# Loading the first MLP rows and weights during the last recurrent segments, and computing six of their products in the free slots of the last block, with two changed priorities

## The chip, the cores and the metric

The kernel runs on one core of one Trainium2 chip. The metric is the device time of one execution in microseconds (us). A run counts as slow when it is over 1.5% above the fastest run of its kernel.

Engines are named as in the profile: PE is TensorE (matmuls), PEld its weight loads, DVE is VectorE, ACT is ScalarE, POOL is GpSimd, SP is the engine that issues the DMA transfers. "L931" is line 931 of the kernel concerned. The lines differ between the two kernels, so a small key goes with each profile.

## The reference, cut to what matters

```python
x = A_x                                            # 1 x 2048 x 512, bfloat16
h = x + A(_layernorm(x), mem0, Wq, Wk, Wv, Wo)     # recurrent attention
h2 = h + B(_layernorm(h), w1, b1, w2, b2)          # MLP 512 -> 1792 -> 512

def A(x, mem, ...):                                # 32 heads of 128
    for s in range(64):                            # 64 segments of 32 tokens
        hs = concat([mem, x[32 * s : 32 * s + 32]])   # 8 memory rows + 32 tokens
        q, k, v = hs @ Wq, hs @ Wk, hs @ Wv
        o = softmax(mask(q @ k.T * scale)) @ v @ Wo
        mem = o[:8]                                # goes on to the next segment
        out[s] = o[8:]

def B(y, ...):
    return gelu(y @ w1 + b1) @ w2 + b2             # gelu: tanh form
```

The attention is a chain of 64 segments that can't overlap freely, because each needs the memory rows of the one before. The MLP of a row needs only that row's `h`, so the MLP of the first rows could start long before the last segment is done. Four segments (128 tokens) make a block, so there are blocks 0 to 15 and block 15 is segments 60 to 63.

Of the kernel before, what the change touches and what calls it, by code (L numbers as in the profile page):

```python
# [24 lines left out]
PHASE = (87, 24, 172, 102)  # L25
HALVES = ("kq", "KA", "QT", "ZCm", "VS", "nmc", "EC", "rsc", "PC", "PTC", "OTm", "KB", "QTB", "VSB")
BONUS = {"EC0": 9.64, "EC1": 2.52, "KA1": 1.19, "KB0": -4.21, "KB1": 40, "OTB": -40, "OTm0": 25.44, "OTm1": -8.14, "OTx": 40, "PA": -3.16, "PC0": 2.46, "PC1":
         4.62, "PTA": -4.05, "PTC0": -40, "PTC1": 2.94, "QT0": -2.59, "QT1": 6.99, "QTB0": 6.21, "QTB1": -0.93, "SA": -13.03, "TT": 6.79, "VBD": 1.92,
         "VS0": 0.75, "VS1": -11.93, "VSB0": -5.47, "VSB1": 15.43, "WK": 40, "WQ": 1.54, "WV": 2.9, "ZCb": 0.16, "ZCm0": 40, "ZCm1": -3.19, "ag":
         -4.83, "ag2": 40, "b1n": 6.73, "b1t": -6.81, "b2bc": 40, "cneg": -40, "hB": 3.99, "hTm": -5.4, "hTx": 5.79, "hd": -2.53, "kq0": 4.71, "kq1":  # L30
         12.67, "kq2": 10.08, "kq5": 6.67, "maskA": -7.3, "maskAF": -11.82, "maskCF": -12.78, "maskL": 40, "maskR": 2.12, "nma": -4.99, "nmc0": 40,
         "nmc1": 40, "oN": -40, "opA": 4.9, "opB": -1.91, "rs": 40, "rs2": -8.34, "rsa": -1.22, "rsc0": -3.89, "rsc1": -3.1, "sma": -4.13, "st2": -40,
         "vd": -1.71, "xT": 0.29, "xn": -0.19, "xr": 3.08}
# [3 lines left out]

# [9 lines left out]
class Op:  # L47
    __slots__ = ("eng", "fn", "reads", "writes", "idx", "gidx", "deps", "sig", "sigcount", "waits",
                 "tag", "pad", "name", "is_dma", "dma_sem", "dur", "mode", "rank", "start", "succ", "prev", "ni", "dma_count", "alts", "kind")

    def __init__(self, eng, fn, reads, writes, name, dur, mode):
# [3 lines left out]
        self.tag = self.pad = None  # L55
# [11 lines left out]
class Sched:  # L67
# [235 lines left out]
    def align(self):  # L303

        at, seg, owed, late = FETCH_AT, 0, 0, 0
        for o in self.streams["pe"]:
            at += len(o.waits) // 2
            if PHASE and o.tag is not None and o.tag[0] != seg:
                seg = o.tag[0]
                owed = (PHASE[seg % 4] - at) % FETCH_N  # L310
                if owed > FETCH_N - SLIP:
                    owed = 0
            if o.pad is not None and owed > 0:
                o.pad[0] = min(owed, PADS)
                owed -= o.pad[0]
            at += o.ni + (o.pad[0] if o.pad is not None else 0)
# [55 lines left out]
P = 128  # L372
# [5 lines left out]
DC = 4  # L378
# [10 lines left out]
MC, MR, MF = 1, 2, 3  # L389

# [25 lines left out]
def build_kernel(nc, A_x, A_mem0, A_Wq, A_Wk, A_Wv, A_Wo, B_w1, B_b1, B_w2, B_b2, out):  # L416
# [3 lines left out]
    with st:  # L420
# [209 lines left out]
        def one_pass(lhs, reads, W, key, r, bank, rhs):  # L630

            for cc in range(DC):
                pad = [0]

                def f(e, cc=cc, pad=pad):
                    for j in range(4):
                        for _ in range(j, pad[0], 4):
                            e.ldweights(lhs(cc), tile_position=(0, 32 * j))
                        ins = e.matmul(ps[bank][32 * j:32 * j + 32, :], lhs(cc), rhs(W, r, cc, j), start=(cc == 0), stop=(cc == DC - 1), tile_position=(0, 32 * j))  # L639
                    return ins  # L640
                S.op("pe", f, reads=[(key, r, cc)] + reads, writes=[("ps", bank)], dur=0.215, mode=MC, ni=8).pad = pad

        def two_passes(lhs, reads, parts):

            for cc in range(DC):
                pad = [0]

                def f(e, cc=cc, pad=pad):
                    for n, (W, _, r, bank, rhs) in enumerate(parts):
                        for j in range(4):  # L650
                            o, l, m = ps[bank][32 * j:32 * j + 32, :], lhs(cc), rhs(W, r, cc, j)
                            if n == 0:
                                for _ in range(4 + j, pad[0], 4):
                                    e.ldweights(l, tile_position=(0, 32 * j))
                            if n == 0 or j < pad[0]:
                                ins = e.matmul(o, l, m, start=(cc == 0), stop=(cc == DC - 1), tile_position=(0, 32 * j))
                            else:
                                ins = matmul_kept(e, o, l, m, cc == 0, cc == DC - 1, (0, 32 * j), (P, 32))
                    return ins
                S.op("pe", f, reads=[(key, r, cc) for _, key, r, _, _ in parts] + reads, writes=[("ps", p[3]) for p in parts], dur=0.43, mode=MC, ni=12).pad = pad  # L660
# [15 lines left out]
        def pack_a(s):  # L676
            sl = s % RING
            return (lambda cc: hT[:, sl, cc, :]), [("hTx", (s // 4) % RBLK), ("hTm", sl)]

        def pack_b(bk):  # L680
            return (lambda cc: hB[:, bk % RBLK, cc, :]), [("hB", bk % RBLK)]
# [45 lines left out]
        def kq_B(bk, qk, r, bank):  # L727
            W, key = WKQ[qk]
            one_pass(*pack_b(bk), W, key, r, bank, cols_kq)
            kq_B_out(bk, qk, r, bank)  # L730

        def v_B(bk, r, bank):
            one_pass(*pack_b(bk), WV, "WV", r, bank, cols_v)
# [245 lines left out]
        hx0, xn0 = xr[:, 2:6, :], view(hT, 4 * DC * SEG, [P, TBS, D])  # L979
        used = {"WQ": [], "WK": [], "WV": []}  # L980

        def hx_of(k):
            return hx0 if k == 0 else hx2[:, k % 2]

        def xn_of(k):
            return xn0 if k == 0 else xn2[:, k % 2]
# [7 lines left out]
        def p2_load(k):  # L994
            after = S.users([("xr", i) for i in range(2, 6)]) if k == 0 else used["WQ"]
            S.dma(lambda e: e.dma_start(hx_of(k), hd[:, k * TBS:(k + 1) * TBS, :]), 512, reads=[("hd", k * TBS + t) for t in range(TBS)],
                  writes=[("hx", bf_of(k))], after=after)

        def p2_norm(k):
            after = S.users([("hTx", i) for i in range(1, RBLK)] + [("hTm", i) for i in range(4, RING)]) if k == 0 else used["WV"]  # L1000
            for t in range(TBS):
                tb = k * TBS + t
                S.op("dve", lambda e, tb=tb, t=t: e.tensor_scalar(xn_of(k)[:, t, :], hx_of(k)[:, t, :], agg2[:, tb, 0:1], rst2[:, tb:tb + 1], ALU.subtract, ALU.mult),
                     reads=[("hx", bf_of(k)), ("ag2", tb), ("rs2", tb)], writes=[("xn4", bf_of(k), t)], after=after, dur=0.4)

        def p2_res(k):

            for t in range(TBS):
                S.op("pool", lambda e, t=t: e.tensor_tensor(hb[:, k % 2, t, :], hx_of(k)[:, t, :], b2bc[:], ALU.add), reads=[("hx", bf_of(k)), "b2bc"],
                     writes=[("hb", k % 2, t)], after=used["WV"] + S.users([("rs2", NTB - 1)]), dur=1.1)  # L1010

        def p2_T(k):
            for t in range(TBS):
                S.dma(lambda e, t=t: e.dma_start_transpose(hnT_of(k)[:, :, t * P:(t + 1) * P], xn_of(k)[:, t, :]), 256, reads=[("xn4", bf_of(k), t)],
                      writes=[("hnT", bf_of(k), t)], after=[] if k == 0 else used["WQ"])
# [8 lines left out]
        ln1(0)  # L1024
        for s in range(NS):
# [7 lines left out]
            if s == NS - 4:  # L1033
                p2_load(0)
                p2_norm(0)
                p2_T(0)

            def part_F2():
                banks = BANK["F0"], BANK["F1"]
                if 0 < bk < NTB - 1 and sg < 3:  # L1040
                    W, key, cols = ((WK, "WK", cols_kq), (WQ, "WQ", cols_kq), (WV, "WV", cols_v))[sg]
                    two_passes(*pack_b(bk + 1), [(W, key, r, banks[r], cols) for r in range(2)])
# [8 lines left out]
            def part_F(r):  # L1051
                if sg < 2 and 0 < bk < NTB - 1:
                    kq_B(bk + 1, sg, r, BANK["F%d" % r])
                if sg == 2 and 0 < bk < NTB - 1:
                    v_B(bk + 1, r, BANK["F%d" % r])
                if sg == 3 and bk > 0 and r == 1:
                    wo_B(bk - 1, BANK["FB"])

            late, done = [], []
# [15 lines left out]
            def part(name):  # L1075
                r = int(name[-1]) if name[-1].isdigit() else 0
                if name in ("K0", "K1"):
                    one_pass(*pack_a(s), WK, "WK", r, bank_of[name], cols_kq)
                    k_seg(s, r, bank_of[name])
                elif name in ("Q0", "Q1"):  # L1080
                    one_pass(*pack_a(s), WQ, "WQ", r, bank_of[name], cols_kq)
                    q_seg(s, r, bank_of[name])
                elif name in ("QK0", "QK1"):
                    two_passes(*pack_a(s), [(WQ, "WQ", r, bank_of["Q%d" % r], cols_kq), (WK, "WK", r, bank_of["K%d" % r], cols_kq)])
                    q_seg(s, r, bank_of["Q%d" % r])
                    k_seg(s, r, bank_of["K%d" % r])
                elif name == "V":
                    two_passes(*pack_a(s), [(WV, "WV", r, bank_of["V%d" % r], cols_v) for r in range(2)])
# [214 lines left out]
```

## The kernel before: what the change and the argument touch

The kernel is not written in the order in which the engines run it. Each operation is recorded, and a static list scheduler then fixes every engine's order before the program is built. An operation is named by the tile that it writes first ("kind"), and a table of priorities, `BONUS`, is added to its rank. The rank is the scheduler's own estimate, in us, of the longest path from the operation to the end.

```python
BONUS = {"EC0": 9.64, ..., "OTB": -40, ..., "st2": -40, ..., "xn": -0.19, "xr": 3.08}
...
        for o in topo:
            o.rank = o.dur + max([self.lat(o, s) + s.rank for s in o.succ], default=0.0)
        def push(o):      # only when all that o depends on has been popped
            heapq.heappush(heap, (-o.rank - BONUS.get(o.kind, 0.0), pos[o], o.gidx, o))
```

So `"OTB": -40` says: give the copies that write the tile OTB their places as if they were 40 us less urgent than they are. PE's own order is fixed by hand, part by part:

```python
ORDER = (("PVA", 0, 99), ("Q0", 0, 4), ("K0", 0, 4), ("Q1", 0, 4), ("K1", 0, 4), ("SC0", 0, 99), ("V0", 0, 4), ("V1", 0, 2), ("SC1", 0, 99), ("SA", 0, 99),
         ("V1", 2, 4), ("F0", 0, 2), ("PV0", 0, 99), ("F0", 2, 4), ("PV1", 0, 99), ("WO", 0, 8), ("F1", 0, 4))
...
            def part_F(r):
                if sg < 2 and 0 < bk < NTB - 1:
                    kq_B(bk + 1, sg, r, BANK["F%d" % r])     # next block's other rows: K, Q
                if sg == 2 and 0 < bk < NTB - 1:
                    v_B(bk + 1, r, BANK["F%d" % r])          # ... and V
                if sg == 3 and bk > 0 and r == 1:
                    wo_B(bk - 1, BANK["FB"])                 # output product of the block before, from OTB
```

`sg` is the segment's place in its block. `F0` and `F1` are filler: PE does the next block's projections there while the softmax of the segment (ACT and DVE) is on its way. Block 15 has no next block, so in segments 60 to 62 these slots are empty.

After a block's output product its rows go through `nat`: transpose, residual, row statistics, and a store to DRAM (`hd`). The input rows `xr` are in a ring of seven blocks:

```python
        def nat(bk):                                          # called at the start of block bk + 2
            S.dma(... dma_start_transpose(oN[:], opT[...]) ...)
            xs = xr[:, bk % XR, :]
            S.op("dve", ... tensor_tensor(xs, xs, oN, ALU.add) ...)
            S.op("dve", lambda e: e.bn_stats(st2[:, i, :], xs), reads=[("xr", bk % XR)], writes=[("st2", i)], ...)
            ...
            S.dma(lambda e: e.dma_start(hd[:, bk, :], xs), ...)
```

The MLP runs in four groups `k` of 512 rows: load the rows, normalize them, transpose them by DMA into `hnT`, multiply by W1 with GELU, multiply by W2. Group 0 borrows a part of the ring, and its load waits for all who use that part:

```python
        hx0, xn0 = xr[:, 2:6, :], view(hT, 4 * DC * SEG, [P, TBS, D])
        def p2_load(k):
            after = S.users([("xr", i) for i in range(2, 6)]) if k == 0 else used["WQ"]
            S.dma(lambda e: e.dma_start(hx_of(k), hd[:, k * TBS:(k + 1) * TBS, :]), 512, ..., after=after)
        def p2_norm(k): ...            # DVE
        def p2_T(k): ...               # four DMA transposes into hnT
        ...
            if s == NS - 4:            # at segment 60
                p2_load(0)
                p2_norm(0)
                p2_T(0)
```

W1 and W2 go into the place of the attention weights, so their loads wait until the last segment no longer needs those (`used["WK"]`), and the tail interleaves what is left of the attention (`rest`) with the first products:

```python
        rest = [lambda: wo(NS, 6, mem=False), lambda: pv_a(NS - 1), ..., lambda: wo(NS + 1, 7, mem=False), lambda: wo_B(NTB - 1, 6), ...]
        for k in range(NSB):
            ...                        # k == 0: one p2_w1 (4 matmuls and a GELU), one piece of rest, eight times
```

## Time and profile before

The median is 883.73 us (three runs, 883.22 to 884.57).

| part of the profiled run | us |
|---|---|
| span | 874.5 |
| start of segment 1 | 54.0 |
| segments 1 to 28 | 308.0 |
| segments 29 to 52 | 269.5 |
| segment 59, with the output product of a block in its F slots | 12.05 |
| segments 60, 61, 62 | 9.85, 11.30, 10.42 |
| start of segment 63 to the end of the span | 132.4 |

The table is worked out from the trace: a segment begins with the first matmul of its part PVA. This profiled run was a quick one: it took 876.2 us, and the timed ones 883 to 885.

Key to the lines of this kernel: L639 projections, L793 scores, L824 probabilities times V, L881 memory part (PVA), L909 output product WO, L1189 W1 products, L1196 W2 products, L948 row statistics of `nat`, L996 load of rows, L1014 transposes into `hnT`, L1207 and L1210 loads of W1 and W2.

First lines of the profile page of the kernel before: the span, the busy time of engines, PE's granted clock in tenths over 40 slices, and the chain of work that ended last.

```profile
span 874.5 us, 50672 instructions
...
PE 792.8 (91%) x22108; PEld 484.7 (55%) x24221; DVE 580.2 (66%) x1877; ACT 547.9 (63%) x1534; POOL 88.2 (10%) x205
...
PEclk9999999999999999999999999999999999789999
...
PE 83%; DVE 8%; issue 4%; DMA 3%; ACT 1%; SPq 1%; ACTq 0%; DVEq 0%
```

PE is busy 91% of the span and is 83% of the chain, so it bounds the kernel on average. The clock row has a hole (7, 8) in slices 35 and 36, around 760 us: this is the seam between the loop and the MLP.

The chain of waits of the kernel before, from 740 to 800 us, in order of time (start, duration, what):

```profile
750.83 1.97 PE ps L909 x67
752.80 2.90 issue
...
758.85 0.70 DVE st L948
...
759.77 1.32 SPq L1014
761.14 4.24 DMA hnT<-hT
...
765.90 1.48 PE ps L1189 x3
767.38 3.04 PE ps L909 x32
...
774.49 1.86 PE ps L909 x64
...
798.28 1.73 PE ps L1189 x8
```

After the last segment's WO (752.80) PE stands for 2.90 us without a wait that the profile shows ("issue"), then finishes 29 matmuls, then waits for the transposed rows. The work after that is slow: 3.04 us for a WO product that takes 1.86 us a little later. At 798.28 the first 512 rows are done and group 1 begins.

PE's waits between 700 and 800 us of the kernel before (who waited for whom, us in total, times, longest):

```profile
PE ps L1189 <- DMA hnT<-hT: 8.7, 1, 8.7
PE ps L909 <- issue: 4.5, 4, 2.9
```

The table of windows of the kernel before, same stretch (window, length, busy time and instructions of each engine, granted clock of PE, share of the DMA engines, GB/s):

```profile
700.00:800.00 100.00, 80.96 (x1896) 49.84 (x2196) 54.31 (x168) 48.58 (x129) 19.15 (x29) 0.93 0.38 93
```

PE is busy for 81 of 100 us here. The idle 19 us, and what is lost at half clock, are all that the change can hope for in this stretch.

### The profile page before, as it was taken

To read this page: it belongs to the slowest core of one execution; us is meant where nothing else is said; L and a number is where in the kernel's file an instruction comes from. 1 tells how busy PE (TensorE), PEld (TensorE's weight loads), DVE (VectorE), ACT (ScalarE), POOL (GpSimd) and SP (SyncE) were. 2 spreads that over 40 slices of the span, in tenths; PEclk is the share of its full clock that TensorE was granted. 3 is DMA by queue.
4 is the path that set the end of the run, shared out by engine and by line. 5 is a ranking of instruction groups with operands and counts; after the bars stand their busy time and mean duration, and the time that the engine had idled before them with its cause. 6 is when DMAs were issued, how large, how long until landed. Compare 5 with 4: busy or idle time off the path is not lost.

```text
span 874.5 us, 50672 instructions
## 1 busy us (share of the span) xinstructions
PE 792.8 (91%) x22108; PEld 484.7 (55%) x24221; DVE 580.2 (66%) x1877; ACT 547.9 (63%) x1534; POOL 88.2 (10%) x205
## 2 busy tenths in 40 slices
PE   3578999999999999999999899989998988499998
PEld 1255666666656665665656565655655655354443
DVE  3267777787777777777777777777877877532111
ACT  2357677777777777776767676767675767334342
POOL 4021000001000100010010001010101000015200
PEclk9999999999999999999999999999999999789999
DMA  9950010101010101010101101010202010951100
GB/s 357 362 168 16 5 28 16 35 17 34 17 34 16 35 16 34 17 34 16 35 22 28 28 22 29 22 34 15 42 17 39 11 40 5 244 96 49 49 24 25
DMA packets 61649, 46.65 MB, mean 53 GB/s; under 512 B 28276, under 2 KB 57852, under 8 KB 61436
## 3 DMA queue, kind: packets, MB, share of 16 engines
q1 hardware_dynamic: 61104, 43.14, 17.8%
q8 instruction: 182, 2.98, 1.4%
q14 instruction: 31, 0.25, 0.1%
q10 hardware_dynamic: 332, 0.27, 0.1%
HBM read 28.98 MB, written 8.39 MB: 43 GB/s over the span
## 4 chain that ended last, share of the span: by engine, by line
PE 83%; DVE 8%; issue 4%; DMA 3%; ACT 1%; SPq 1%; ACTq 0%; DVEq 0%
PE ps L639 44%; PE ps L909 18%; PE ps L1189 6%; PE quad L1196 6%; PE quad L824 4%; PE quad L793 2%; PE quad L881 2%; DVE PC L812 2%; DVE nma L862 1%; DVE nmc L802 1%; DMA WQ<-in_A_Wq_dram 1%; DMA xr<-in_A_x_dram 1%; DVE PTC L813 1%; PE ps L852 1%; PE quad L828 1%
## 5 line engine op out<-in xcount | busy, mean ns | idle before, releaser
L639 PE MATMUL ps<-WQ,hT 128*32 128x512 bf16 x2048 | 137.7, 382 | 4.4 <-DVE hT L915 3.9
L639 PE MATMUL ps<-WK,hT 128*32 128x512 bf16 x2048 | 135.2, 379 | 0.1
L639 PE MATMUL ps<-WV,hT 128*32 128x512 bf16 x2016 | 133.6, 380 | 0.0
L909 PE MATMUL ps<-WO,OT 128*32 128x256 bf16 x4224 | 129.6, 276 | 0.0
L667 ACT ACTIVATE kq<-ps 128x512 bf16<-128x512 f32 x160 | 95.3, 595 | 49.2 <-PE ps L639 42.9
L666 ACT CAST OT<-quad 128x768 bf16<-128x768 f32 (+1 forms) x151 | 74.1, 490 | 80.0 <-PE quad L881 58.7
L666 ACT CAST kq<-ps 128x512 bf16<-128x512 f32 x160 | 93.5, 584 | 39.2 <-PE ps L639 34.6
L909 PEld LDWEIGHTS ps<-WO,OT 128*32 128x32 bf16 x4224 | 107.9, 98 | 7.3 <-issue 1.7
L689 DVE STREAM_TRANSPOSE KALL<-kq 128x256 f32<-128x256 f32 x160 | 71.3, 445 | 29.8 <-ACT kq L666 24.3
L806 ACT ACTIVATE EC<-quad,nmc 128x64 f32<-128x64 f32 x252 | 76.9, 310 | 16.2 <-DVE nmc L802 15.5
L689 DVE STREAM_TRANSPOSE QT<-kq 128x256 f32<-128x256 f32 x128 | 56.8, 444 | 44.2 <-ACT kq L667 43.2
L1192 ACT ACTIVATE WQ<-ps,b1t 128x512 bf16<-128x512 f32 x56 | 38.5, 687 | 75.8 <-PE ps L1189 75.8
L639 PEld LDWEIGHTS ps<-WK,hT 128*32 128x32 bf16 x2048 | 60.6, 97 | 42.6
L710 POOL COPY ZC<-QTB 128x256 bf16<-128x256 bf16 x64 | 25.6, 401 | 485.2 <-PE quad L793 455.3
L666 ACT CAST VS<-ps 128x512 bf16<-128x512 f32 x127 | 74.0, 583 | 0.1
L639 PEld LDWEIGHTS ps<-WQ,hT 128*32 128x32 bf16 x2048 | 56.3, 95 | 28.9 <-issue 2.7
L824 PEld LDWEIGHTS quad<-PTC,VS 32*128 32x128 bf16 x2048 | 25.7, 91 | 69.2 <-ACT OT L666 24.9
L639 PEld LDWEIGHTS ps<-WV,hT 128*32 128x32 bf16 x2016 | 51.0, 95 | 22.9 <-issue 0.2
L1244 DVE TENSOR_TENSOR WV<-quad,WV 128x512 bf16<-128x512 f32 x16 | 11.1, 691 | 73.2 <-PE quad L1196 73.2
L909 PE MATMUL ps<-WO,OTB 128*32 128x256 bf16 x1024 | 42.1, 276 | 16.4 <-issue 16.3
L824 PE MATMUL quad<-PTC,VS 32*128 32x16 bf16 x2048 | 37.5, 168 | 20.6 <-DVE rsc L809 7.6
L1196 PE MATMUL quad<-WK,WQ 128*128 128x512 bf16 x221 | 54.2, 379 | 0.2
(116 smaller groups left out, 1262.8 us busy)
## 6 DMA issues: line engine op xcount, KB each, us to landing
WV<-in_A_Wv_dram SPq DMA_DIRECT2D x4, 1024.0 KB, 9.1
WK<-in_A_Wk_dram SPq DMA_DIRECT2D x4, 1024.0 KB, 17.1
v_last<-VSB SPq DMA_DIRECT2D x64, 64.0 KB, 2.1
WQ<-in_A_Wq_dram SPq DMA_DIRECT2D x4, 1024.0 KB, 9.1
VBD<-v_last SPq DMA_DIRECT2D x64, 64.0 KB, 2.0
WO<-in_A_Wo_dram SPq DMA_DIRECT2D x4, 1024.0 KB, 12.8
WK<-in_B_w_dram SPq DMA_DIRECT2D x4, 896.0 KB, 6.7
h_mid<-xr SPq DMA_DIRECT2D x16, 128.0 KB, 1.8
```

The lines of the kernel that those rows point to most:

```text
L639: ins = e.matmul(ps[bank][32 * j:32 * j + 32, :], lhs(cc), rhs(W, r, cc, j), start=(cc == 0), stop=(cc == DC - 1), tile_position=(0, 32 * j))
L666: return {"act": (lambda e: e.copy(out, src), t_act(n, ps_)), "dve": (lambda e: e.tensor_copy(out, src), 0.16 + 1.042e-3 * n * fast)}
L667: return {"act": (lambda e: e.mul(out, src, scale_), t_act(n, ps_)), "dve": (lambda e: e.tensor_scalar(out, src, scale_, None, ALU.mult), ...
L689: S.op("dve", lambda e: e.transpose(out, src), reads=[("kq", i)], writes=[key], dur=t_dve(256) + 0.02)
L710: S.op("pool", lambda e: e.tensor_copy(dst, src), reads=[("QTB", bk % 2, q) for q in range(2)], writes=[("ZCb", par)], dur=0.45)
L793: ins = e.matmul(o[32 * j:32 * j + 32, 64 * sl:64 * sl + 64], ZC[:, par, h, :], rhs, start=False, stop=(i == 3), tile_position=(0, 32 * j) ...
L806: ins = e.activation(EC[:, r, sl, :], o[:, 64 * sl:64 * sl + 64], ACTF.Exp, bias=nmc[:, r, sl:sl + 1], accum_out=smc[:, r, sl:sl + 1])
L824: e.matmul(quad[:, j, (4 * r + i) * 16:(4 * r + i) * 16 + 16], VS[rows, s % 3, r, i * E:(i + 1) * E], PTC[rows, r, c0:c0 + 16, i // 2], st ...
L909: ins = e.matmul(ps[bank][32 * j:32 * j + 32, 0:256], lhs(slot(h)), wo_cols(h, b), start=(k == 0), stop=(k == 15), tile_position=(0, 32 * ...
L1189: ins = e.matmul(ps[bank][:, 0:SBT], W1[:, cc, fc * P:(fc + 1) * P], hnT_of(k)[:, cc, :], start=(cc == 0), stop=(cc == DC - 1))
L1192: S.op("act", lambda e: e.activation(gT[:, fc, :], ps[bank][:, 0:SBT], ACTF.Gelu_apprx_tanh, bias=b1t[:, fc:fc + 1], scale=1.0), reads=[(" ...
L1196: S.op("pe", lambda e: e.matmul(quad[:, t, :], gT[:, fc, t * P:(t + 1) * P], W2[:, fc, :], start=(fc == 0), stop=(fc == FC - 1)), reads=[( ...
```

## The change

The intent: nothing of the first 512 rows' MLP has to wait for the last segment. Rows 0 to 511 are loaded, normalized and transposed in segments 53 to 56 (an entry of `EARLY` for segment s names a place on PE's order within segment s-1). W1 comes in seven pieces of 256 KB, from segment 56 on, into buffers that are already dead. Six of the fourteen W1 products of these rows fill the empty F slots of segments 60 to 62. The diff, cut; left out are a refactoring of `one_pass` and `two_passes` with a switch (`KEEP = False`) that is off, and the views of the dead buffers.

```diff
-BONUS = {..., "OTB": -40, ..., "xn": -0.19, ...}
+BONUS = {..., "OTB": -3, ..., "gT0": 20, ..., "xn": -10, ...}
+EARLY = {54: (("hx", 0, 0.1), ("hx", 1, 0.6)), 55: (("hn", 0, 0.1), ("hn", 1, 0.4), ("hx", 2, 0.8)), 56: (("hx", 3, 0.3), ("hn", 2, 0.7)),
+         57: (("hn", 3, 0.1), ("w1", 0, 0.6)), 58: (("w1", 6, 0.2),), 59: (("w1", 1, 0.1), ("w1", 2, 0.8)), 60: (("w1", 3, 0.2), ("w1", 4, 0.5), ("w1", 5, 0.8))}
...
+        def hx_early(t, after): ...    # load 128 rows into xT, normalize them into xn
+        def hn_early(t, after): ...    # transpose them into hnT0
+        def w1_early(p, after): ...    # load 256 columns of W1 into homes[p]
+        def w1_first(fc, bank):
+            for cc in range(DC):
+                S.op("pe", ... e.matmul(ps[bank][:, 0:SBT], v[:, c, ...], hnT0[:, cc, :], ...) ...)
+            S.op("act", lambda e: e.activation(g[:, fc % 2, :], ps[bank][:, 0:SBT], ACTF.Gelu_apprx_tanh, bias=b1t[:, fc:fc + 1], scale=1.0), ...)
...
-            if s == NS - 4:
-                p2_load(0)
-                p2_norm(0)
-                p2_T(0)
+            for what, i, name in EARLY.get(s, ()):
+                here = [S.pe_order[at_seg + int(name * (len(S.pe_order) - at_seg))]]
+                {"hx": hx_early, "hn": hn_early, "w1": w1_early}[what](i, here)
...
             def part_F(r):
+                if bk == NTB - 1 and sg < 3:
+                    w1_first(2 * sg + r, BANK["F%d" % r])
...
         pieces = []
-        (the two halves of W1, then the two of W2, then p2_load(1))
+        (the two halves of W2, p2_load(1), p2_load(0), the two halves of W1, p2_norm(1), p2_T(1))
+        for fc in range(6, FC):
+            w1_first(fc, (4, 5)[fc % 2])
+            rest[fc - 6]()
```

Two numbers in the priority table come with it.

## The prediction

> **What bounds the kernel now.** TensorE. The page gives PE matmul 91% of the 874.5 us span, and the chain of waits is 83% PE. In the loop (100 to 700 us, table of windows) PE is busy 572 of 600 us. The weak place is the seam between the loop and the MLP. The chain of waits shows block 15's segments at 10.4, 11.3, 10.4 and 9.9 us, against 12.06 us with work in the F slots; with empty slots PE waits about 2.8 us a segment. At 752.80 PE stalls 2.90 us ("issue", while W1 and W2 load), and from 757.19 it waits 8.71 us for the four transposes of hnT (ended by the DMA hnT<-hT). After that PE is slow: three MLP matmuls take 1.48 us (0.65 when warm) and a 64-matmul WO product 3.04 us (1.86 when warm). The first 512 rows end at 798.28.
>
> **What the change does.** Rows 0 to 511 are loaded, normalized and transposed in segments 54 to 57; seven W1 pieces of 256 KB are loaded in segments 57 to 60 into dead buffers. Six of the fourteen W1 products (4 matmuls of 0.216 us each, 0.86 us) go into the free F slots of segments 60 to 62.
>
> Gain, all on PE's chain:
> - the wait for hnT: 8.7 us
> - slow PE after it: 0.8 + 1.2 = 2.0 us
> - six products moved out of the tail: 6 x 0.86 = 5.2 us
> - small waits: about 0.6 us
>
> Together 16.5 us. The tail from WO of segment 63 to the end of the first 512 rows falls from 45.5 to about 29 us. The 2.9 us issue stall stays.
>
> Cost:
> - The slots are not quite free (changes of tile shape): 0.4 us x 3 = 1.2 us.
> - ACT tables. Before, all Exp come first and the profile shows one table load for Gelu (1283 ns, at 751.58). Now two Gelu (0.69 us) per segment stand between Exps, so each of three segments gets at least two loads, perhaps four if the first Gelu lands ahead of the SA exponential. The Trainium skill ("ScalarE: Activation LUTs", "What ACT_TABLE_LOAD costs") gives about 1283 ns and a drain of about 1380 ns; the trace agrees on the first and shows no drain. The reload for Exp stands just ahead of EC, which PV0 waits for, so most of it is exposed: I estimate 1.5 to 3 us a segment, 6 us.
> - Early DMA among the loop's loads and instruction fetches, and the changed priorities: 1 us, uncertain in sign.
>
> Net 16.5 - 1.2 - 6 - 1 = about 8.5 us faster, 1%.
>
> **Predicted time: 875.0 us, range 866.0 to 881.0.** Faster by over 2%: 0.07; within 2%: 0.91; slower by over 2%: 0.02.
>
> **What would show the steps.** Right: no wait of several us for hnT after the last WO; full clock in the tail; the first 512 rows' W2 products ending some 8 us earlier; 6 to 12 more table loads on ACT between 710 and 755 us; block 15's segments longer by 1.5 to 3.5 us, with PE waiting for EC or PTC; segments before 54 unchanged. Wrong: block 15 at its old length (loads hidden: gain near 15 us), or longer by over 4 us each (nothing left).
>
> **What would make it wrong.** No table loads, or hidden ones (865 to 868). Four loads a segment with a drain each (880 or more). A larger instruction stall when the tail's PE work meets the W2 and W1 loads. Loop segments moved by the new priority of the OTB copy: 0.1 us a segment would be 6 us either way.

## More of the kernel before

The buffers `xr[:, 2:6]` last held the rows of blocks 9, 10, 11 and 12.

The timeline of DVE in the kernel before (start, duration, line, operation):

```profile
699.09 0.69 DVE L948 BATCH_NORM_STATS2 st<-xr 128x6 f32<-128x512 bf16 x1
...
742.87 0.70 DVE L948 BATCH_NORM_STATS2 st<-xr 128x6 f32<-128x512 bf16 x1
```

The timeline of SP, the issuing engine, in the kernel before:

```profile
743.65 0.34 SPq L996 DMA_DIRECT2D xr<-h_mid  x1
...
756.16 7.01 SPq L1014 DMA_TRANSPOSE hnT<-hT  x4
```

Counted back from the sixteenth and last of these instructions, the statistics at 699.09 are block 9's and those at 742.87 block 12's. The load of rows 0 to 511 follows 0.08 us after the latter's end at 743.57, and the transposes follow from it.

## The result, and the profile after

The changed kernel takes 869.28 us (median of four runs, 867.04 to 871.54) against 883.48 for the kernel before (883.01 to 884.57). The ratio of fast runs is 0.9838, with a 95% interval of 0.9803 to 0.9872: faster by 1.6%, within the class "within 2%". A later repeat (experiment 12) gave 862.23 against 877.26 us, ratio 0.9837 (0.9802 to 0.9872). A ratio here is the mean time of one kernel's fast runs over the mean of the other's in the same rounds, so it is not quite the ratio of the medians quoted.

Key to the lines of this kernel: L670 projections, L815 scores, L846 probabilities times V, L903 PVA, L931 WO, L1069 W1 products of the first 512 rows and L1073 their GELU, L828 the exponential EC of the segment, L688 copies by ACT, L1260 and L1267 W1 and W2 products of the rest.

The same lines of the page, kernel after:

```profile
span 869.8 us, 50658 instructions
...
PE 800.3 (92%) x22121; PEld 492.4 (57%) x24182; DVE 576.8 (66%) x1870; ACT 555.6 (64%) x1547; POOL 87.5 (10%) x205
...
PEclk9879999999999999999999999999999999999999
...
PE 85%; DVE 6%; issue 4%; DMA 3%; ACT 2%; SPq 0%; ACTq 0%; DVEq 0%
```

The hole in the clock at the seam is gone from the row of slices, though not wholly, as the next view shows. The chain of waits of the kernel after, between 716 and 800 us:

```profile
731.39 1.28 ACT L828
732.68 0.70 ACT EC L828 x4
...
759.35 1.97 PE ps L931 x67
761.32 4.02 issue
...
766.37 1.82 PE ps L1069 x4
768.19 2.63 PE ps L931 x43
...
793.63 4.50 PE ps L1260 x20
```

From WO of segment 63 (761.32) to the end of the first 512 rows (793.63) it is 32.3 us, against 45.5 us before (752.80 to 798.28). But WO of segment 63 ends 8.5 us later than it did (in part because the first profile of the kernel before was quick up to there; the table below has the stages). Three things are new on the chain: a 1.28 us item of ACT ahead of EC, a stall of 4.02 us instead of 2.90, and, after the stall, slow PE work again (1.82 us for four matmuls of W1 that take 0.97 later on).

PE's waits between 700 and 800 us, kernel after:

```profile
PE ps L931 <- issue: 5.6, 2, 4.0
PE ps L1069 <- ACT VS L688: 1.9, 2, 1.0
PE quad L846 <- ACT EC L828: 1.2, 1, 1.2
```

The wait for `hnT` is gone; waits for ACT have come. The table of windows, kernel after:

```profile
700.00:800.00 100.00, 91.01 (x2034) 53.35 (x2311) 55.13 (x169) 58.71 (x139) 17.21 (x21) 0.97 0.31 92
```

The 1.28 us item is named by the timeline of ACT, kernel after:

```profile
723.86 1.28 ACT L1073 ACT_TABLE_LOAD   x1
725.15 0.69 ACT L1073 ACTIVATE xn<-ps,b1t 128x512 bf16<-128x512 f32 x1
...
730.78 0.59 ACT L688 CAST kq<-ps 128x512 bf16<-128x512 f32 x1
731.39 1.28 ACT L828 ACT_TABLE_LOAD   x1
732.68 0.31 ACT L828 ACTIVATE EC<-quad,nmc 128x64 f32<-128x64 f32 x1
```

A change of function table stands between the exponential of SA (the scores of the memory part) and the first GELU, and another between the GELUs and the next segment's exponential. The second delays EC, on which PE's next part depends. Two loads a segment, not four. The Trainium skill ("ScalarE: Activation LUTs", "What ACT_TABLE_LOAD costs") gives about 1283 ns for the load, which agrees with 1.28 us, and a drain of about 1380 ns; here there is no room for a drain, since the load begins 0.02 us after the copy before it ends and the exponential begins 0.01 us after the load. The measurement decides: a change of table costs 1.28 us.

Stage by stage (worked out from the traces as before; "before, again" is the second profile of the kernel before, whose span, 883.1 us, is more like its timed runs):

| us | before | before, again | after | after, again |
|---|---|---|---|---|
| segments 1 to 28 | 308.0 | 311.3 | 311.0 | 309.8 |
| segments 29 to 52 | 269.5 | 274.0 | 268.4 | 264.4 |
| segment 59 | 12.05 | 12.09 | 13.77 | 11.34 |
| segments 60 + 61 + 62 | 31.6 | 31.2 | 34.7 | 34.3 |
| segment 63 to the end | 132.4 | 132.2 | 119.5 | 118.8 |
| span | 874.5 | 883.1 | 869.8 | 859.8 |

The total agrees with what I predicted (875, range 866 to 881), and so does a large gain at the end. Two rows don't fit my reasons: segments 29 to 52, which the early loads don't touch, seem shorter, and block 15 costs 3 us, not 7. The experiments go after both.

### The profile page after: what moved, and what is told of

Read it like the earlier page. It is cut to its first block, busy times and chain, and to the rows that moved or that the text cites. A ratio compares the mean times of both kernels' runs of the same rounds, so it can differ in the third digit from the quotient of the medians.

```text
span 869.8 us, 50658 instructions
## 1 busy us (share of the span) xinstructions
PE 800.3 (92%) x22121; PEld 492.4 (57%) x24182; DVE 576.8 (66%) x1870; ACT 555.6 (64%) x1547; POOL 87.5 (10%) x205
## 4 chain that ended last, share of the span: by engine, by line
PE 85%; DVE 6%; issue 4%; DMA 3%; ACT 2%; SPq 0%; ACTq 0%; DVEq 0%
PE ps L670 45%; PE ps L931 19%; PE quad L1267 6%; PE ps L1260 4%; PE quad L846 4%; PE quad L903 2%; PE quad L815 2%; PE ps L1069 2%; DVE PC L834 1%; DMA WQ<-in_A_Wq_dram 1%; DVE nma L884 1%; DVE nmc L824 1%; DMA xr<-in_A_x_dram 1%; PE ps L874 1%; PE quad L850 1%
## 5 line engine op out<-in xcount | busy, mean ns | idle before, releaser
L670 PE MATMUL ps<-WQ,hT 128*32 128x512 bf16 x2048 | 140.2, 382 | 3.3 <-DVE hT L937 2.3
L670 PE MATMUL ps<-WK,hT 128*32 128x512 bf16 x2048 | 137.9, 379 | 0.3 <-issue 0.3
L670 PE MATMUL ps<-WV,hT 128*32 128x512 bf16 x2032 | 136.1, 381 | 0.0
L931 PE MATMUL ps<-WO,OT 128*32 128x256 bf16 x4224 | 130.6, 277 | 0.0
L688 ACT CAST OT<-quad 128x128 bf16<-128x128 f32 (+1 forms) x147 | 73.1, 497 | 81.0 <-PE quad L903 56.4
L688 ACT CAST kq<-ps 128x512 bf16<-128x512 f32 x160 | 93.4, 583 | 34.6 <-PE ps L670 34.5
L931 PEld LDWEIGHTS ps<-WO,OT 128*32 128x32 bf16 x4224 | 108.4, 98 | 7.6 <-issue 1.7
L670 PEld LDWEIGHTS ps<-WK,hT 128*32 128x32 bf16 x2048 | 64.0, 97 | 39.9
L828 ACT ACTIVATE EC<-quad,nmc 128x64 f32<-128x64 f32 x252 | 77.1, 311 | 13.0 <-DVE nmc L824 12.9
L670 PEld LDWEIGHTS ps<-WQ,hT 128*32 128x32 bf16 x2048 | 57.6, 95 | 31.0 <-issue 5.3
L688 ACT CAST VS<-ps 128x512 bf16<-128x512 f32 x127 | 74.1, 584 | 0.0
L670 PEld LDWEIGHTS ps<-WV,hT 128*32 128x32 bf16 x2032 | 54.6, 96 | 21.9 <-issue 1.8
L846 PEld LDWEIGHTS quad<-PTC,VS 32*128 32x128 bf16 x2048 | 25.8, 91 | 66.2 <-ACT OT L688 24.6
L931 PE MATMUL ps<-WO,OTB 128*32 128x256 bf16 x1024 | 42.7, 276 | 21.8 <-issue 21.7
L1263 ACT ACTIVATE WQ<-ps,b1t 128x512 bf16<-128x512 f32 x42 | 28.9, 688 | 51.9 <-PE ps L1260 51.9
L846 PE MATMUL quad<-PTC,VS 32*128 32x16 bf16 x2048 | 38.6, 168 | 15.8 <-DVE rsc L831 5.8
L815 PEld LDWEIGHTS quad<-KALL,ZC 128*32 128x32 bf16 x2016 | 36.5, 96 | 25.5 <-DVE KALL L711 14.2
```

The lines of the kernel that those rows point to most:

```text
L670: ins = e.matmul(o, l, m, start=(k == 0), stop=(k == DC - 1), tile_position=(0, 32 * j), skip_group_check=True)
L688: return {"act": (lambda e: e.copy(out, src), t_act(n, ps_)), "dve": (lambda e: e.tensor_copy(out, src), 0.16 + 1.042e-3 * n * fast)}
L815: ins = e.matmul(o[32 * j:32 * j + 32, 64 * sl:64 * sl + 64], ZC[:, par, h, :], rhs, start=False, stop=(i == 3), tile_position=(0, 32 * j) ...
L828: ins = e.activation(EC[:, r, sl, :], o[:, 64 * sl:64 * sl + 64], ACTF.Exp, bias=nmc[:, r, sl:sl + 1], accum_out=smc[:, r, sl:sl + 1])
L846: e.matmul(quad[:, j, (4 * r + i) * 16:(4 * r + i) * 16 + 16], VS[rows, s % 3, r, i * E:(i + 1) * E], PTC[rows, r, c0:c0 + 16, i // 2], st ...
L931: ins = e.matmul(ps[bank][32 * j:32 * j + 32, 0:256], lhs(slot(h)), wo_cols(h, b), start=(k == 0), stop=(k == 15), tile_position=(0, 32 * ...
```

## The experiments

There were twelve runs; two of them repeat the given kernels. Kernels are compared only within the same rounds. The theories are these.

- T1, as predicted: the gain is the early rows (no wait for `hnT`) plus the six products moved, less the table loads.
- T2: the gain is mostly the two priorities, which change the order of instructions everywhere; the early rows and the slots add little.
- T3: what the change leaves on the table is the table loads, or T3': the instruction stalls beside the bulk loads.

### 1. The kernel before, a second time

No edit.

> The kernel before, unchanged, for a second profile. Its first profile took 876.2 us though its timed runs took 883.0 to 884.6. If the profiled execution was an odd one, this profile lasts about 882 us and shows where 7 us more go (expected: longer issue stalls or more half-clock stretches). If profiling itself shortens it, 876 again.

The run took 884.85 us, span 883.1 us; its state is unknown, being single, so it serves as a profile and not as a time. Compared with the first profile, segments 1 to 28 are 3.3 us longer and segments 29 to 52 4.5 us longer, with the same instructions in the same order. In the stretch at the end the two agree to 0.2 us. So the first profile was a quick one in its loop, and the "4.7 us between the spans" of the two main profiles understates the 14.2 us between the timed medians.

### 2. Early rows and early W1, but no work in the slots

```diff
             def part_F(r):
-                if bk == NTB - 1 and sg < 3:
-                    w1_first(2 * sg + r, BANK["F%d" % r])
...
-        for fc in range(6, FC):
+        for fc in range(FC):
             w1_first(fc, (4, 5)[fc % 2])
-            rest[fc - 6]()
+            if fc < len(rest):
+                rest[fc]()
```

> The change without the slot filling: rows and W1 pieces still come early, all fourteen products run in the tail, no Gelu among the Exps. Theory A (the seam gives most of the gain; slot filling saves 5.2 us and gives back about 3.9 us in block 15): about 870.5 us, 1.3 us slower than the change, block 15 segments back at about 10.4 us, one Gelu table load. Rival B (slot filling is the gain): 874 us or more. Rival C (slot filling loses): 867 us or less.

Measured: 866.69 us (865.22 to 868.66, five runs) against 880.45, ratio 0.9843 (0.9813 to 0.9872), correct. The whole change has 0.9838. So filling the slots, the headline of the change, brings nothing that these runs can tell from zero. In the profile the bookkeeping is visible: from segment 63 to the end it takes 126.3 us, 6.8 us more than in the change, and segments 60 to 62 take 31.0 us, 3.6 us less. The 3.2 us between the two are within what the intervals leave open (some 3 us either way), and a part of them is chance: the stall after WO of segment 63 was 4.8 us long in this profile.

### 3. The slots' GELUs replaced by exponentials

```diff
-            S.op("act", lambda e: e.activation(g[:, fc % 2, :], ps[bank][:, 0:SBT], ACTF.Gelu_apprx_tanh, ...), ...)
+            S.op("act", lambda e: e.activation(g[:, fc % 2, :], ps[bank][:, 0:SBT], ACTF.Exp if fc < 6 else ACTF.Gelu_apprx_tanh, ...), ...)
```

The result is wrong (relative error 0.249); what is wanted is the time with the same work and no change of table in block 15.

> The change with the six slot Gelus computed as Exp (wrong result on purpose): same instructions, same shapes, no change of table inside block 15. Theory A (each reload of the Exp table ahead of EC is exposed, about 1.2 us in segments 61, 62 and 63): about 865.7 us, 3.5 us under the change, segments 61 and 62 at about 10.6 us in place of 11.8. Rival (the loads hide and the longer segments come from the slot matmuls): 869 us and segments still at 11.8 us.

Measured: 862.62 us (861.97 to 864.36, five runs) against 880.45, ratio 0.9797 (0.9765 to 0.9829). Against 0.9838 that is 0.4% of 880 us, about 3.6 us, for the table loads. Segments 60 to 62 take 32.75 us.

### 4. The slots' GELUs held back until the exponentials are over

```diff
+            if fc < 6:
+                S.either(copy2(g[:, fc % 2, :], ps[bank][:, 0:SBT], 512), ...)      # DVE or ACT, no table
+                return
...
+        def gelu_late(fc):             # in place, in the tail
+            S.op("act", ... e.activation(g[...], g[...], ACTF.Gelu_apprx_tanh, bias=b1t[:, fc:fc + 1], ...),
+                 ..., after=S.users(["SA", ("EC", 0), ("EC", 1)]), dur=0.69)
```

> A correct way to the same: in the slots ACT only copies the sums to bf16 (as long as a Gelu, needs no table), and the six Gelus run in place in the tail after the last Exp. Theory A: as the run with Exp, about 865.7 us (3.5 us under the change), since ACT is mostly idle in the tail. Rival: the six late Gelus (0.69 us each) hold up the W2 products and take it back: 868 us or more.

Measured: 861.74 us (861.27 to 864.24, five runs) against 880.45, ratio 0.9791 (0.9761 to 0.982), correct. This is the same gain as with the exponentials, this time with the right result: about 4 us. Segments 60 to 62 take 32.3 us, 1.3 us more than with empty slots. The Trainium skill's advice to group work by table set ("ScalarE: Activation LUTs", "Table sets: the hidden batching unit") holds here, with 4 us for three exposed reloads.

So T3 has a number: the reloads cost 3.6 to 4.1 us in all, about 1.2 us for each of the three that stand ahead of EC. I had put them at 6. Each of the two intervals still overlaps that of the change (0.9803 to 0.9872) at its edge; what carries the point is that two kernels agree, and that segment 62 takes 10.65 us in both profiles, against 11.78 in both profiles of the change.

### 5. The kernel before with the two new priorities and nothing else

```diff
-BONUS = {..., "OTB": -40, ..., "xn": -0.19, "xr": 3.08}
+BONUS = {..., "OTB": -3, ..., "xn": -10, "xr": 3.08}
```

> The kernel before with only the two priorities of the change (the OTB copy from -40 to -3, the xn work from -0.19 to -10), which reorder ACT, DVE and the DMA queue in the whole loop. In the profiles segments 29 to 53, which the change should not touch, took 269.5 and 274.0 us before and 264.4 to 268.4 us in the change and its variants. If the priorities make that: 4 to 5 us faster than before, a ratio of about 0.995, segments 29 to 53 near 266 us. Rival (that stretch only varies from run to run): ratio 0.999 to 1.001.

Measured: 867.66 us (866.29 to 868.42, six runs) against 881.33, ratio 0.9854 (0.9831 to 0.9878), correct. The whole change has 0.9838 and 0.9837. Two numbers in a table, with no early load and no filled slot, bring a gain of 1.46%, where the whole change brings 1.62%. T1 as the sole account is dead.

Comparing the order of instructions of kernels that were built but not run makes it one number: with `xn` alone at -10 the program is the same as the kernel before, instruction for instruction, and with `OTB` alone at -3 it is the same as this one.

Where it comes from, first: the seam. The timelines of DVE and of SP in the kernel before with the new priorities:

```profile
687.79 0.65 DVE L948 BATCH_NORM_STATS2 st<-xr 128x6 f32<-128x512 bf16 x1
```

```profile
704.97 1.93 SPq L1014 DMA_TRANSPOSE hnT<-hT  x1
...
711.23 4.32 SPq L1014 DMA_TRANSPOSE hnT<-hT  x3
```

Block 12's statistics run at 687.79 instead of 742.87, the rows' buffers come free, and the transposes of rows 0 to 511 are issued from 704.97 instead of 756.16. No wait for `hnT` is left; from segment 63 to the end it takes 126.7 us instead of 132.4. The 8.7 us wait of the kernel before was a buffer hold through a late, low-priority statistics instruction.

Second: the loop. PE's waits between 365 and 634 us in the kernel before (segments 29 to 52):

```profile
PE quad L793 <- DVE ZC L703: 2.5, 5, 0.5
PE quad L824 <- issue: 2.3, 4, 0.6
```

and between 366 and 631 us in the kernel before with the new priorities:

```profile
PE quad L824 <- issue: 0.4, 1, 0.4
```

A wait of 0.5 us for DVE in the first segment of five blocks is gone, and so is most of a stall inside L824: 2.5 + 1.9 = 4.4 us, and the stretch is 4.4 us shorter (265.1 against 269.5). On DVE's timeline the cause of the first is plain: in the kernel before the statistics of incoming rows (L584, 0.65 us) and their normalization (L588, 0.41 us) stand between the segment's own transposes, and the transpose that the scores need begins at 579.25; with the new order those two are elsewhere. The first segments of the blocks mostly take 12.05 us before and 10.9 to 11.2 after.

How a lower urgency of the OTB copies comes to push the statistics back, I read from the scheduler and haven't shown: PE's order is a chain, the output product of the block needs OTB, and what hangs behind it in the scheduler's heap is placed late, after other things have taken the places.

### 6. The change with the old priorities

```diff
-BONUS = {..., "OTB": -3, ..., "gT0": 20, ..., "xn": -10, "xr": 3.08}
+BONUS = {..., "OTB": -40, ..., "gT0": 20, ..., "xn": -0.19, "xr": 3.08}
```

> The change with those two priorities put back. If they are worth 4 to 5 us: a ratio to before of about 0.989 in place of the change's 0.984. Rival: 0.984.

Measured: 867.69 us (864.58 to 876.45, six runs) against 881.33, ratio 0.9868 (0.9829 to 0.9907), correct. This was a surprise to both sides. T1 is not simply false: the structure alone brings 1.3% as well. The two parts overlap, because both end the same 8.7 us wait: together they bring 1.6%, not 2.8%. Its interval and the change's overlap for the most part, so what the priorities add to the structure can't be told from zero by the clock. In the profile the loop is as slow as before (272.2 us in segments 29 to 52, and the first segments of the blocks have their 12.06 us again; the three kernels with the new priority that ran on the same chip have 265.0 to 266.4 us), and the end is among the shortest of all, 115.0 us.

That 115.0 against 119 in the change has a cause of its own. PE's waits between 700 and 800 us in this kernel:

```profile
PE ps L931 <- issue: 3.0, 3, 1.2
```

The stall after WO of segment 63 was 0.92 us here, not 4.02. Four of the six bulk loads stand where they stand in the change, counted from the end of WO (both halves of W2, one half of W1 and one load of rows); but the other load of rows and the other half of W1, issued at 759.86 and 762.07 in the change, came only at 771.97 and 774.03. So the length of that stall depends on something that the order of the program moves, and fewer bulk loads stood beside it. The next runs are about it.

### 7. The later W1 pieces moved out of segment 59

```diff
-         ..., 59: (("w1", 1, 0.1), ("w1", 2, 0.8)), 60: (("w1", 3, 0.2), ("w1", 4, 0.5), ("w1", 5, 0.8))}
+         ..., 59: (("w1", 1, 0.1),), 61: (("w1", 2, 0.1), ("w1", 3, 0.6)), 62: (("w1", 4, 0.2), ("w1", 5, 0.7))}
```

> The change with W1 pieces 2 to 5 loaded in segments 60 and 61 in place of 58 and 59. In the change's profile segment 59 takes 13.77 us against 12.05 before: an issue stall of 1.55 us beside these loads and the V transfers, then half clock for 3.4 us. If the loads lengthen the instruction fetch: segment 59 back near 12.1 us, no half clock there, 1 to 1.7 us faster than the change, ratio about 0.982, unless the loads do the same to the segments they move to. Rival (the stall has nothing to do with the loads): segment 59 stays near 13.7.

Measured: 862.82 us (861.89 to 864.49, six runs) against 881.33, ratio 0.9800 (0.9775 to 0.9825), correct. Segment 59 takes 11.76 us instead of 13.77. What it removes is seen in the change's own profile: PE's waits between 700 and 716 us, and the table of windows just after them.

```profile
PE ps L931 <- issue: 1.6, 1, 1.6
```

```profile
711.70:715.10 3.40, 3.40 (x72) 2.73 (x67) 1.47 (x5) 0.36 (x1) 0.00 (x0) 0.50 0.52 153
```

In segment 59 four pieces of W1 are issued, from 705.2 to 712.4 us. A stall of 1.6 us among them (708.45 to 710.00) is followed, from 711.71 us, by 3.4 us at half the clock (0.50). A stall of 1.8 us at the same place in experiment 4 was not, so the one doesn't always bring the other. The intervals of 0.9800 and 0.9838 overlap (the latter reaches from 0.9803), and in the repeat of the change segment 59 took only 11.34 us, so the collision doesn't come in every run; I call the gain of some 3 us likely and not shown.

### 8. The bulk loads held until after WO of segment 63

```diff
+        pieces = []                    # earlier
...
+        used["WK"].append(S.pe_order[-1])      # W2, W1: not before PE's last work of segment 63
...
-                      writes=[("hnT", bf_of(k), t)], after=used["WQ"])
+                      writes=[("hnT", bf_of(k), t)], after=used["WQ"] + pieces[3:])
```

> The change with the whole W2 and W1 loads held until the last matmul of segment 63, and the transposes of rows 512 to 1023 after them. Theory (the 4.0 us issue stall after WO of segment 63 is an instruction fetch queued behind these loads, and it brings the half clock): the stall under 1 us and no half clock after it, 3 to 4.5 us faster, ratio about 0.980. Rival 1 (the stall is a fetch boundary, whatever loads): still 4 us, ratio 0.984. Rival 2: the stall only moves to the next fetches in the tail, or W2 comes too late: 0.984 or more.

Measured: 861.22 us (859.28 to 864.46, six runs) against 881.33, ratio 0.9787 (0.976 to 0.9814), correct. The chain of waits of this kernel at the same place:

```profile
754.48 0.99 issue
...
756.51 0.97 PE ps L1070 x4
757.48 1.86 PE ps L931 x64
```

The stall is 0.99 us instead of 4.02 or 3.49, and the slow work behind it (1.82 and 2.63 us in the change) is back at 0.97 and 1.86: 3.0 + 0.85 + 0.77 = 4.6 us against the change's first profile; segment 63 to the end takes 114.8 us instead of 119.5. The interval overlaps the change's at the edge (0.9803 to 0.9814), but the profile shows the two things that were expected to go, gone. The cure works by moving the loads, so the long stall needs them; that they alone make it is not shown. What PE waits for in it is not a semaphore that the profile shows. In the change the next 16 KB packet of the larger of the two DMA queues for instructions (taken here for PE's) moves in the middle of it, from 762.76 to 763.79, while the DMA engines are nearly full; that fits a late fetch of instructions. The other traces say the same: in all fourteen profiles this stall, between 0.5 and 4.8 us long, ends 1.2 to 1.6 us after such a packet has landed (1.55 in the change, 1.40 here, 1.47 in experiment 6, where the packet came before WO ended), though the packets are 3.5 to 9 us apart. No run changed the fetch by itself, so this is strong evidence and not a test.

### 9. The kernel before, with only the statistics of four blocks made urgent

```diff
-            S.op("dve", lambda e: e.bn_stats(st2[:, i, :], xs), ..., writes=[("st2", i)], ...)
+            stats = S.op("dve", lambda e: e.bn_stats(st2[:, i, :], xs), ..., writes=[("st2", i)], ...)
+            if 9 <= bk <= 12:
+                stats.kind = "st2early"        # BONUS["st2early"] = 0, instead of -40
```

The straightforward test of the buffer hold would have been a separate buffer for rows 0 to 511; there are 520 bytes left in the on-chip memory of each partition (the builder says so when it is asked for more), and it takes 4 KB, so it couldn't be built without taking another buffer away. Instead, this run removes what the hold waits for.

> The kernel before with one thing changed: the row statistics of blocks 9 to 12 get the priority 0 in place of -40, so that they no longer run as late as segment 63; the loop up to segment 59 keeps its order. Theory: in before, the load of rows 0 to 511 waits for these statistics (they read the buffer that it fills; the last ran at 742.87 us and the load was issued at 743.65), and that is the whole cause of the 8.7 us wait for hnT. Then the load and the transposes come more than 15 us earlier, the wait for hnT is gone without any early loads, and from segment 63 to the end of the first 512 rows it takes about 51 us in place of 56; segments 60 and 61 may lengthen by 1 to 2 us in exchange; ratio about 0.995. Segments 29 to 53 stay at 269 to 274 us, so the rest of what the new priority gave (ratio 0.985) is in the loop. Rival (the wait comes from the place in the program where the load is issued): the wait stays, ratio 1.000.

Measured: 868.34 us (861.84 to 873.67, six runs) against 875.42, ratio 0.9921 (0.9885 to 0.9958), correct. SP's timeline in this kernel:

```profile
712.93 0.46 SPq L998 DMA_DIRECT2D xr<-h_mid  x1
...
718.72 6.67 SPq L1016 DMA_TRANSPOSE hnT<-hT  x4
```

The load moves from 743.65 to 712.93, the wait for `hnT` is gone, the end takes 124.3 us instead of 132, and the loop (269.1 us in segments 29 to 52) is as before. So the hold by the statistics was the cause of the wait, and it is worth 0.8%, about 7 us; the rest of the OTB effect is the loop.

### 10 and 11. The cures together, with and without work in the slots

The first takes the change with edits 4, 7 and 8 (late GELU, later pieces, held loads); the second takes edit 2 (no slots) with edits 7 and 8.

```diff
  (change) + late GELU + later pieces + held bulk loads       ->  "best"
  (change) - slots     + later pieces + held bulk loads       ->  "seam_best"
```

> The change with three repairs together: the six slot Gelus in the tail, W1 pieces 2 to 5 in segments 60 and 61, and the big W2 and W1 loads held until segment 63 is through. Alone they gave ratios of 0.979, 0.980 and 0.979 against the change's 0.984. If they add: 3.5 + 1.5 + 4 us under the change, about 0.974, 858 us. If they overlap (the same stall repaired twice): about 0.977.

> The same repairs without the slot filling (all fourteen products in the tail; nothing to defer). This shows what the slots are worth once no table load stands between the Exps: six products of 0.86 us move out of the tail and cost about 0.3 us a segment, so this should be about 4 us slower than the run with slots, ratio about 0.979. Rival (slots worth nothing even then): the same.

Measured: best 853.95 us (852.46 to 854.93, four runs), ratio 0.9752 (0.9734 to 0.9769), correct; seam_best 861.05 us (854.04 to 864.82, six runs), ratio 0.9829 (0.9798 to 0.9861); the kernel before 875.42 in both. The first beats both given kernels. PE's waits and the table of windows of best, 700 to 800 us:

```profile
PE ps L931 <- issue: 1.6, 3, 0.6
```

```profile
700.00:800.00 100.00, 98.06 (x1935) 56.44 (x2178) 53.64 (x163) 55.98 (x137) 17.70 (x22) 1.00 0.36 99
```

PE is busy 98 of 100 us at full clock, against 81 before and 91 in the change. Segments 60 to 62 take 32.5 us with full slots and no table loads.

The pair was also meant to give the worth of the slots once the tables are out of the way, and it doesn't give it cleanly. seam_best had a stall of 2.8 us at 743 us, beside two loads of 512 KB, with half the clock after it, some 4.5 us in all. The ratios differ by 0.77%, or 6.7 us; less 4.5 us, 2.2 us of it may be the slots. That is left open.

### 12. The change, a second time

No edit.

> The change once more, in 5 rounds, because its first ratio (0.9838, interval 0.9803 to 0.9872) is too wide to set beside the run with the new priorities alone (0.9854) and the run without slots (0.9843). If the early loads and the slots add next to nothing to the priorities: 0.983 to 0.986 again. If they do add: 0.982 or less. A second profile should again show block 15's segments 61 and 62 at about 11.8 us with one reload of the Exp table in each, an issue stall of 3 to 5 us after WO of segment 63, and half clock after it.

Measured: 862.23 us (859.71 to 866.94, six runs) against 877.26 us, ratio 0.9837 (0.9802 to 0.9872), correct. The ratio repeats to 0.0001, though both times are 6 to 7 us lower there. In this profile the stall after WO was 3.49 us, and segment 59 took 11.34.

## Why the prediction was right or wrong

The time was right: 875.0 predicted with a range of 866 to 881, 869.28 measured; "within 2%" at 0.91 was the right class. The sum behind it was right in part, and by luck in another part.

| term, as predicted | predicted, us | what the runs showed |
|---|---|---|
| the wait for `hnT` goes | 8.7 | goes, but the new priority alone ends it too (5), and so do the statistics alone (9: about 7 us) |
| slow PE after it goes | 2.0 | 0.4: after a 4.0 us stall the half clock is back, 1.82 for 0.97 and 2.63 for 1.86 us |
| six products out of the tail | 5.2 | 6.8 to 7.5 less from segment 63 to the end than with empty slots (2) |
| "The 2.9 us issue stall stays" | 0 | 4.0 and 3.5 in the two profiles of the change; 1.0 with the loads held (8) |
| slots not quite free | -1.2 | 1.3 and 1.7 without table loads (4 and 3 against 2): about right |
| table loads | -6 | 3.6 to 4.1 (3 and 4), two a segment, only the reload for EC exposed, no drain |
| early DMA and "the changed priorities: 1 us, uncertain in sign" | -1 | the priorities alone: 1.46% of 881 us, a gain of 12.9 us (5) |

**The step that failed** is the last one, "the changed priorities: 1 us, uncertain in sign", and with it the reading that the 8.7 us wait needs the early rows to go. I had written the right warning ("Loop segments moved by the new priority of the OTB copy: 0.1 us a segment would be 6 us either way") but gave it no weight. I read from the chain that PE waited for the transposes, and that the transposes were issued late; I did not follow SP's load back to what released it. The runs showed a buffer hold in its place: with the statistics of four blocks made urgent, and nothing else, the load moves from 743.65 to 712.93 us and the wait is gone (9). The chain of waits itself names the statistics instruction L948, at 758.85, but that is block 13's; the timeline of DVE, with block 12's at 742.87 and the load of rows 0.08 us after its end, is the view that shows the hold.

**Why the total still came out.** The gain was 14.2 us by the medians, against 8.5 predicted; the range held it, but not for the reasons given, and that much was luck. The sum was not further off because the terms overlap. The structure alone brings 0.9868 (6), and the priorities alone bring 0.9854 (5), but together they bring 0.9838: what the one has taken, the other can't. My sum of 8.5 us is the structure's gain, and for the structure alone that is near the truth: 1.32% of 881 us is 11.6 us, and its interval reaches from 8 to 15. The further 3 us of the whole change are within the noise of these two ratios; in the profiles the loop gains 4 to 8 us by the priority and the end, with its longer stall, gives about 4 back. The loop I had expected unchanged ("segments before 54 unchanged": wrong; segments 29 to 52 take 264 to 268 us in kernels with the new priority and 269 to 274 without).

**Where the slots' gain went.** PE's work did move. In the profiles some 7 us leave the end; 3.6 to 4.1 us go to the table loads, 1.3 to 1.7 us to the slots themselves, and the stalls beside the early and bulk loads hide the rest. Timed, the change with slots (0.9838) and without (0.9843) can't be told apart. The loss is recoverable: without the table loads the same slots bring 0.9791, and with the loads moved as well 0.9752.

**Block 15's segments.** I had counted on "12.06 us with work in the F slots" against 10.4 with none, so on almost 3 us of idle PE. The 12.06 belongs to a segment with the output product of a whole block, or, before the new priority, to the first of a block with its DVE wait. Ordinary segments with full slots take 10.6 to 10.9 us. The slots are nearly free of cost for that reason, and empty ones save only 0.4 to 0.6 us a segment on average (1.3 to 1.7 us over the three).

**What stays open.** Why a lower urgency of OTB delays the statistics in the scheduler's placing. Whether the "issue" stalls are late fetches of instructions: they end 1.2 to 1.6 us after a packet of instructions in every profile, the long ones have bulk loads beside them, and they shrink where fewer of these loads do (6, 8), but no run changed the fetch alone. Which stall brings the half clock: not each one did. And what the slots are worth by themselves.

## What to carry to other kernels

When a diff brings a new structure and a changed number in a priority table, cost the number by its own run: here one entry (OTB, from -40 to -3), run by itself, gave nine tenths of the gain of the whole, and the structure without it eight tenths, so that neither number could have been had from the run of both. Before you pay for an early load, follow the late one back to what released it; a low-priority instruction that nobody seems to wait for may hold the buffer. Work put into a free slot of PE brings its other engines' needs with it (here a change of ACT's function table, 1.28 us each), so hold back the part that changes the table, and keep bulk loads away from the places where PE has no slack.

## What the Trainium skill lacked or had wrong

- "ScalarE: Activation LUTs", "What ACT_TABLE_LOAD costs": the page has about 1283 ns and about 1380 ns of drain, 2.66 us for a change of table. The load took 1.28 us, began 0.02 us after the copy before it ended, and the exponential began 0.01 us after it: no drain. Timed, three exposed reloads cost 3.6 to 4.1 us in all.
- "Runtime: NRT & Kernel Launch", "Instruction fetch mechanics": the page calls the crossing of a 16 KiB block of instructions "mostly hidden". Here PE stood 2.9 to 4.8 us with nothing shown to wait for, beside bulk loads, with a 16 KB packet of the instruction queue moving in the middle (from 762.76 us in the change); in experiment 6, with two of the loads later, it was 0.9 us, and with the loads moved the stall was 1.0 and 0.5 us in two kernels, 2.8 in a third (seam_best). In all fourteen profiles it ended 1.2 to 1.6 us after such a packet landed. The page doesn't say that bulk loads can expose the fetch; that the stall is the fetch is likely and not tested by itself.
- "TensorE: Matmul & The Clock Gate", "Part 1: The HAM clock gate (the "warmup" mystery)": the page has the half rate after at least one idle window of about 3.4 us. The lengths agree (the half-clock stretches between 700 and 800 us are 3.4, 6.8 or 13.7 us), but one came after a stall of only 1.6 us, at 711.7 us in the change, while stalls of 1.8 us (experiment 4, at 708.7), 3.9 us (experiment 5, at 750.9) and 3.4 us (experiment 9, at 753.1) had none just after them.
- No page has it that one and the same program differs from set to set of runs (four of the sets are on chips 2, 3, 5 and 8; chip and hour can't be told apart): the medians of the kernel before were 875.4, 877.3, 880.5, 881.3 and 883.5 us in the five sets of timed runs, a spread of 0.9%, and within one set its runs reached from 874.3 to 881.7. That is more than most of the effects studied here, so only ratios of one set of rounds decide.
